# The half-size token block of the last stage: first instead of last, and the last drain in two halves

## The chip, the cores and the metric

The kernel runs on one core of one Trainium2 chip. The metric is the device time of one execution in microseconds (us). A core has a matrix engine (TensorE, called PE in the profile; its weight loads are PEld), VectorE (DVE), ScalarE (ACT), GpSimd (POOL) and a queue engine (SyncE, SP), which issues the transfers between the chip's memory (DRAM) and the on-chip buffers; 16 DMA engines carry them. Each engine works through its own instructions in order and waits for others by semaphores.

## The reference

An attention layer feeds a gated layer, and that feeds a second feed-forward layer. Only the last product of the second feed-forward layer is touched by the change.

```
def _moe2_ref(x, w_in, w_out) -> np.ndarray:
    h = x @ w_in
    g = h - np.tanh(h)
    return (g @ w_out).astype(np.float32)
```

Here x has 2304 tokens x 512, w_in is 512 x 2048 and w_out is 2048 x 512; all is float32.

## The kernel before

The program has a chain of stages: attention with the gated layer's first products, the gated layer's output product, the product `x @ w_in` with the tanh (function `hmm`), and last the product `g @ w_out`, which starts 855.74 us into the span and is called the last stage here. Products are made in pieces: each float32 operand is split into a high and a low part, and three matmuls (high by high, high by low, low by high) replace one.

**The last stage** uses a seven-product scheme for 2 x 2 blocks (Strassen's, in Winograd's form): rows 0 to 1151 and rows 1152 to 2303 of the tokens are the two block rows, the two halves of the 2048 inner columns and of the 512 outer columns are the other blocks. The tokens of each half are cut into blocks `s` of `TB` = 256, of which there are `NSB` = 5: four of 256 and one of 128, since 1152 = 4 x 256 + 128. The inner columns are cut into `MP` = 8 chunks `p`. A step is one pair (s, p); steps run over p inside s, 40 in all, and are numbered 0 to 39 here in the order in which they run.

A step of a 256-token block makes 42 matmuls (7 products x 2 token groups of 128 x 3 matmuls, lines 1023 to 1025), one of the 128-token block 21. The seven products of a block gather in seven PSUM banks over the eight steps, in the order 1, 2, 6, 7, 5, 4, 3. At a block's eighth step `drain` empties each bank as soon as its product is complete: bank 1 by an ACT copy (line 994), the others by seven DVE additions (line 979), of which four are results; `ostore` (line 984) stores those four. The next block's products start in the same banks, so they wait for these drains.

Each step needs prepared operands: `sprep` makes them two steps ahead. `sload` (line 916, three transfers on SP) brings four blocks of g from DRAM into a tile `g2` (two buffers); `sprep` then forms sums on POOL (lines 929, 931) and DVE (lines 930, 933), the high parts `sh` on ACT (lines 932 for the first three operands, 935 for the other four) and the low parts `sl` on DVE (lines 934 and 936). `sh` and `sl` have two buffers each, so ACT's line 932 for step i+2 waits until PE has finished step i. At its end `sprep` calls `sload` for two steps later still, which takes the `g2` buffer that line 934 was the last to read. The first two calls of `sprep` come during the end of the stage ahead, and the loop calls it once behind each step's matmuls (and drains).

**The weights** of w_out lie converted in DRAM, 1792 KB for each p. Those of p = 0 to 2 stay on the chip from earlier; those of p = 3 to 7 are fetched by `wload` (line 942) into memory that the stage ahead gives up, four during its last 16 of 20 products and that of p = 7 behind its last one. They share the SP queue with the loads of g and with the stores of h (line 893), from which g is read back.

Of the kernel before, what the change touches and what calls it, by code (L numbers as in the profile page):

```python
# [13 lines left out]
ALU = mybir.AluOpType  # L14

B, H, S, D = 4, 8, 576, 64
NT, DM = B * S, H * D
# [26 lines left out]
TB = 256  # L44
DG = 2
NSB = -(-(NT // 2) // TB)
# [18 lines left out]
def attention_moe_moe2(ctx: ExitStack, tc: tile.TileContext, kqT, v, s, wg, wv, wo, win, wo2, out):  # L65
    nc = tc.nc
    PE, ACT, DVE, POOL, SP = nc.tensor, nc.scalar, nc.vector, nc.gpsimd, nc.sync
# [169 lines left out]
    g2scr = [dram.tile([128, NT], F, name=f"h{m}") for m in range(M2)]  # L237
# [424 lines left out]
    for i in range(n + LN + 2):  # L662
        u, t = steps[i] if i < n else (None, None)
        b, G, h = units[u] if i < n else (None, None, None)
        first = i < n and t == GRP[G][2][0]
        k = min(share.pop(0) if share and i < n else 1, len(mq))
# [48 lines left out]
        elif i < n and G == 1:  # L715
            s = t - 2 if h % 2 == 0 else t
# [117 lines left out]
    for i, (blk, m) in enumerate(order):  # L834
        w = BLKS[blk][1]
# [5 lines left out]
        for d in range(KD):  # L841
            c = slice(d * 128, d * 128 + 128)
            PE.matmul(acc[d], won[m][0][:, c], gh, start=(m == 0), stop=False)  # L843
            PE.matmul(acc[d], won[m][1][:, c], gh, start=False, stop=False)  # L844
        for d in range(KD):
            c = slice(d * 128, d * 128 + 128)
# [30 lines left out]
    def hmm(i):  # L877
# [14 lines left out]
        DVE.tensor_tensor(out=th, in0=ps, in1=th, op=ALU.subtract)  # L892
        SP.dma_start(out=g2scr[MO[j]][:, a:a + w], in_=th)

    def dwidth(s):
        return min(TB, NT // 2 - s * TB)

    def d_open():
        cv_left.close()
        DP["g"] = ctx.enter_context(tc.tile_pool(name="dg", bufs=2, side="left"))  # L900
        DP["s"] = ctx.enter_context(tc.tile_pool(name="ds", bufs=2, side="right"))
        for i in range(DG):
            sload(i)

    def sload(i):
        if i >= NSB * MP:
            return
        s, p = divmod(i, MP)
        tb = dwidth(s)
        g = S_["g", i] = DP["g"].tile([128, 4, TB], F, tag="g2", name="g2", bufs=DG)  # L910
        for f, (m, t0) in enumerate(((p, NT // 2), (p, 0), (p + MP, 0), (p + MP, NT // 2))):
            if f == 3:
                continue
            k = 2 if f == 2 else 1
            src = g2scr[m].rearrange("p (a t) -> p a t", a=2)[:, t0 // (NT // 2):t0 // (NT // 2) + k, s * TB:s * TB + tb]
            SP.dma_start(out=g[:, f:f + k, 0:tb], in_=src)

    def sprep():
        i = S_["i"]
        if i >= NSB * MP:  # L920
            return
        S_["i"] += 1
        tb = dwidth(i // MP)
        g = S_.pop(("g", i))[:, :, 0:tb]
        t = DP["g"].tile([128, 4, TB], F, tag="s4", name="s4", bufs=2)[:, :, 0:tb]
        sh = DP["s"].tile([128, 7, TB], R, tag="sh", name="sh")[:, :, 0:tb]
        sl = DP["s"].tile([128, 7, TB], R, tag="sl", name="sl")[:, :, 0:tb]
        a21, a11, a12, a22 = (g[:, f] for f in range(4))
        POOL.tensor_tensor(out=t[:, 0], in0=a21, in1=a22, op=ALU.add)  # L929
        DVE.tensor_tensor(out=t[:, 2], in0=a11, in1=a21, op=ALU.subtract)  # L930
        POOL.tensor_tensor(out=t[:, 1], in0=t[:, 0], in1=a11, op=ALU.subtract)
        ACT.activation(out=sh[:, 0:3], in_=g[:, 1:4], func=AF.Copy)  # L932
        DVE.tensor_tensor(out=t[:, 3], in0=a12, in1=t[:, 1], op=ALU.subtract)
        DVE.tensor_tensor(out=sl[:, 0:3], in0=g[:, 1:4], in1=sh[:, 0:3].bitcast(F), op=ALU.subtract)  # L934
        ACT.activation(out=sh[:, 3:7], in_=t, func=AF.Copy)
        DVE.tensor_tensor(out=sl[:, 3:7], in0=t, in1=sh[:, 3:7].bitcast(F), op=ALU.subtract)
        sload(i + DG)
        S_["s", i] = sh, sl
# [31 lines left out]
    op = ctx.enter_context(tc.tile_pool(name="op", bufs=1, side="left"))  # L970
    acc = {}

    def otile(k, w):
        pool = w2 if k[1:].isdigit() else fp if k[0] == "t" else op
        return pool.tile([128, 512], F, tag=k, name="o")[:, 0:w]

    def dadd(k, x, y, w, op=ALU.add):
        o = otile(k, w)
        DVE.tensor_tensor(out=o, in0=x, in1=y, op=op)
        return o  # L980

    def ostore(s, lo_tok, half, o, w):
        r0 = (0 if lo_tok else NT // 2) + s * TB
        SP.dma_start(out=out[r0:r0 + w // 2, half * 256:half * 256 + 256].rearrange("(a p) c -> p a c", p=128),
                     in_=o.rearrange("p (a c) -> p a c", c=256))

    R_ = {}

    def drain(s, n, w):
        par = s % 2  # L990
        a = acc[n]
        if n == 1:
            R_["c1"] = otile("o00", w)
            ACT.activation(out=R_["c1"], in_=a, func=AF.Copy)
        elif n == 2:
            ostore(s, True, 0, dadd(("th0", "th1")[par], a, R_["c1"], w), w)
        elif n == 6:
            R_["u2"] = dadd("o01", a, R_["c1"], w)
        elif n == 7:
            R_["u3"] = dadd("o10", a, R_["u2"], w)  # L1000
        elif n == 5:
            ostore(s, False, 1, dadd(("th2", "th3")[par], a, R_["u3"], w), w)
            R_["v"] = dadd("o11", a, R_["u2"], w)
        elif n == 4:
            ostore(s, False, 0, dadd(("th4", "th5")[par], a, R_["u3"], w), w)
        else:
            ostore(s, True, 1, dadd(("ox0", "ox1")[par], a, R_["v"], w), w)

    wload(MP - 1)
    for i, (s, p) in enumerate(dsteps):  # L1010
        tb = dwidth(s)
        nt = tb // 128
        if p == 0:
            for n in OORD:
                acc[n] = bank(n, [128, nt * 256])
        sh, sl = S_.pop(("s", i))
        w = WO[p]
        for n in OORD:
            g, f = OG[n], OW[n]
            for t in range(nt):  # L1020
                o = acc[n][:, t * 256:t * 256 + 256]
                c = slice(t * 128, t * 128 + 128)
                PE.matmul(o, sh[:, g, c], w[:, 0, f], start=(p == 0 and t == 0), stop=False)  # L1023
                PE.matmul(o, sh[:, g, c], w[:, 1, f], start=False, stop=False)  # L1024
                PE.matmul(o, sl[:, g, c], w[:, 0, f], start=False, stop=(p == MP - 1 and t == nt - 1))  # L1025
            if p == MP - 1:
                drain(s, n, nt * 256)
        sprep()
# [43 lines left out]
```

## Time and profile before

| | |
|---|---|
| time, three runs | 1042.85, 1043.33 (median), 1045.74 us |
| profiled execution: its time, its span | 1044.35 us, 1042.6 us |
| PE busy in the span | 1018.2 us (98%) |
| matmuls of the last stage | 3 x 504 = 1512, from 855.74 to 1038.57 us |
| last DVE instruction ends | 1039.71 us |

The page of the profile gives each engine's busy time, and the trace behind it is read by views: rows of time, waits, windows, transfers. The profiled execution's time is 1.75 us longer than its span, which lies around the program, and 1.02 us above the median of the three runs. Times in the rows count from the start of the span. A name such as `g<-h` reads "tile g is written from tensor h".

### The profile page before, as it was taken

The page shows a single profiled execution, that of the slowest core. Times are in us where ns is not written, and L with a number is a line of the kernel's source. Part 1 is how long each engine was busy: PE and PEld are TensorE (multiplying, and loading weights), DVE is VectorE, ACT ScalarE, POOL GpSimd, SP SyncE. Part 2 cuts the span into 40 slices and gives each one's busy share as a digit, 9 for nine tenths or more (in the row PEclk, how much of TensorE's full clock was granted, in tenths as well). Part 3 has the DMA queues.
Part 4 walks back from the last instruction along what each step waited for, and adds up shares of the span by engine and source line. Part 5 has one row for each costly group of instructions (what it writes and reads, how often), then busy time and mean ns, then how long its engine had stood idle before and what let it go on. Part 6 is the DMA issues. An engine that isn't in the chain of part 4 may idle for free.

```text
span 1042.6 us, 19611 instructions
## 1 busy us (share of the span) xinstructions
PE 1018.2 (98%) x6812; PEld 950.6 (91%) x6812; DVE 636.9 (61%) x1467; ACT 513.6 (49%) x1178; POOL 458.1 (44%) x608
## 2 busy tenths in 40 slices
PE   7898999999999999999999999999999999999997
PEld 5688999999999999999988888888888889999997
DVE  5787667677666566646533444365565245887876
ACT  5876656677656665634432333344444233434333
POOL 3678555677666565513200000055565103453452
PEclk8999999999999999999999999999999999999999
DMA  6674457576565655307634332365787696534433
GB/s 199 212 249 134 131 132 201 163 203 175 165 179 157 166 160 166 105 32 240 217 102 131 112 116 76 117 212 176 263 302 273 245 325 219 151 112 135 145 96 102
DMA packets 109091, 177.09 MB, mean 170 GB/s; under 512 B 16000, under 2 KB 71296, under 8 KB 107712
## 3 DMA queue, kind: packets, MB, share of 16 engines
q1 hardware_dynamic: 108992, 175.85, 54.1%
q8 instruction: 53, 0.87, 0.3%
q14 instruction: 46, 0.38, 0.1%
HBM read 128.79 MB, written 47.00 MB: 169 GB/s over the span
## 4 chain that ended last, share of the span: by engine, by line
PE 88%; DMA 3%; DVE 3%; POOL 2%; issue 2%; ACT 1%; SPq 1%; DVEq 0%; POOLq 0%; ACTq 0%
PE bank L577 9%; PE bank L573 9%; PE bank L574 9%; PE bank L886 6%; PE bank L885 6%; PE bank L889 6%; PE bank L515 5%; PE bank L843 5%; PE bank L844 5%; PE bank L847 5%; PE bank L1025 5%; PE bank L1024 5%; PE bank L1023 5%; PE bank L470 4%; PE bank L411 1%
## 5 line engine op out<-in xcount | busy, mean ns | idle before, releaser
L1025 PE MATMUL bank<-wo,sl 128*128 128x256 f32 x504 | 142.5, 283 | 1.7 <-DVE sl L934 1.5
L1023 PE MATMUL bank<-wo,sh 128*128 128x256 f32 x504 | 141.8, 281 | 0.0
L1024 PE MATMUL bank<-wo,sh 128*128 128x256 f32 x504 | 141.7, 281 | 0.0
L886 PE MATMUL bank<-y,ring 128*128 128x512 f32 (+1 forms) x320 | 115.8, 368 | 0.0
L885 PE MATMUL bank<-y,ring 128*128 128x512 f32 (+1 forms) x320 | 115.7, 368 | 0.0
L892 DVE TENSOR_TENSOR th<-bank,th 128x512 f32<-128x512 f32 (+1 forms) x80 | 50.2, 635 | 92.2 <-ACT th L891 87.9
L115 POOL TENSOR_TENSOR ring<-tmp,ring 128x512 fp32r<-128x512 f32 x16 | 22.7, 1421 | 185.4 <-ACT ring L125 165.2
L494 ACT ACTIVATE pth<-bank 128x384 fp32r<-128x384 f32 (+1 forms) x96 | 45.5, 474 | 113.0 <-PE bank L470 93.0
L1025 PEld LDWEIGHTS bank<-wo,sl 128*128 128x128 f32 x504 | 95.2, 189 | 2.8 <-DVE sl L934 2.1
L929 POOL TENSOR_TENSOR s<-g 128x256 f32<-128x256 f32 (+1 forms) x40 | 34.9, 873 | 140.9 <-DMA g<-h 127.6
L495 DVE TENSOR_TENSOR ptl<-bank,pth 128x384 fp32r<-128x384 f32 (+1 forms) x96 | 51.2, 534 | 72.8 <-ACT pth L494 72.2
L1024 PEld LDWEIGHTS bank<-wo,sh 128*128 128x128 f32 x504 | 95.2, 189 | 0.0
L1023 PEld LDWEIGHTS bank<-wo,sh 128*128 128x128 f32 x504 | 95.2, 189 | 0.0
L800 DVE TENSOR_TENSOR gl<-g,gh 128x512 fp32r<-128x512 f32 (+1 forms) x60 | 37.7, 637 | 84.7 <-PE bank L847 61.9
L438 ACT ACTIVATE sp<-sp,nm 128x128 f32<-128x128 f32 (+4 forms) x144 | 83.4, 579 | 5.3 <-DVE nm L431 5.2
L891 ACT ACTIVATE th<-bank 128x512 f32<-128x512 f32 (+1 forms) x80 | 43.4, 551 | 79.0 <-PE bank L889 76.3
L470 PE MATMUL bank<-ident,sp 128*128 128x128 f32 x400 | 68.4, 275 | 11.5 <-POOL sp L454 4.6
L799 ACT ACTIVATE gh<-g 128x512 fp32r<-128x512 f32 (+1 forms) x60 | 35.0, 591 | 90.4 <-PE bank L844 79.6
L889 PE MATMUL bank<-y,ring 128*128 128x512 f32 (+1 forms) x320 | 78.7, 368 | 0.0
L932 ACT ACTIVATE sh<-g 128x768 fp32r<-128x768 f32 (+1 forms) x40 | 31.2, 780 | 86.6 <-PE bank L1024 59.5
L342 POOL TENSOR_TENSOR kl<-kq,kh 128x576 fp32r<-128x576 f32 (+1 forms) x48 | 57.6, 1200 | 29.7 <-ACT kh L341 29.0
L886 PEld LDWEIGHTS bank<-y,ring 128*128 128x128 f32 x320 | 60.3, 189 | 10.2
(385 smaller groups left out, 3169.4 us busy)
## 6 DMA issues: line engine op xcount, KB each, us to landing
h<-th SPq DMA_DIRECT2D x64, 256.0 KB, 2.6
kq<-in_kq SPq DMA_DIRECT2D x32, 448.0 KB, 3.7
raw<-in_wo SPq DMA_DIRECT2D x28, 512.0 KB, 5.0
g<-g SPq DMA_DIRECT2D x48, 256.0 KB, 2.7
g<-h SPq DMA_DIRECT2D x72, 128.0 KB, 2.3
w<-wst SPq DMA_DIRECT2D x5, 1792.0 KB, 6.3
wo<-w SPq DMA_DIRECT2D x5, 1792.0 KB, 8.6
cbc<-cum SPq DMA_DIRECT2D x32, 256.0 KB, 5.2
```

Of the source, the lines that this page charges most:

```text
L342: POOL.tensor_tensor(out=kl, in0=d["k"], in1=kh.bitcast(F), op=ALU.subtract)
L438: ACT.activation(out=e["sp"], in_=e["sp"], func=AF.Exp, scale=-1.0, bias=e["m"], accum_out=e["sum"])
L470: PE.transpose(e["tr"][j // 4][:, j % 4, :], e["sp"][:, c:c + 128], ident)
L573: PE.matmul(ps, wh[:, c], xh[:, k], start=(k == 0), stop=False)
L574: PE.matmul(ps, wl[:, c], xh[:, k], start=False, stop=False)
L577: PE.matmul(ps, wh[:, c], xl[:, k], start=False, stop=(k == KD - 1))
L885: PE.matmul(ps, wh[:, c], yh[k], start=(k == 0), stop=False)
L886: PE.matmul(ps, wl[:, c], yh[k], start=False, stop=False)
L889: PE.matmul(ps, wh[:, c], yl[k], start=False, stop=(k == KD - 1))
L1023: PE.matmul(o, sh[:, g, c], w[:, 0, f], start=(p == 0 and t == 0), stop=False)
L1024: PE.matmul(o, sh[:, g, c], w[:, 1, f], start=False, stop=False)
L1025: PE.matmul(o, sl[:, g, c], w[:, 0, f], start=False, stop=(p == MP - 1 and t == nt - 1))
```

## The change

The block of 128 tokens becomes block 0, and blocks 1 to 4 have 256. `dstart(s)` gives the first token of a block. So steps 0 to 7 now have 21 matmuls and load 64 KB blocks of g where they had 42 and 128 KB, and steps 32 to 39 have 42 where they had 21. The last drain of the last block, which is now 512 columns wide, is made as two additions of 256 columns, each with a store of its own. Beside that one more addition and one more store, the number of operations, the order in which each engine takes them, and the weight transfers stay as they were. Line numbers from 895 to 1010 rise by 5 or so, and those of the last loop by 10.

```diff
+    short = NT // 2 % TB
+
     def dwidth(s):
-        return min(TB, NT // 2 - s * TB)
+        return TB if s else short
+
+    def dstart(s):
+        return s * TB - (TB - short) * (s > 0)
...
-            src = g2scr[m].rearrange("p (a t) -> p a t", a=2)[:, t0 // (NT // 2):t0 // (NT // 2) + k, s * TB:s * TB + tb]
+            src = g2scr[m].rearrange("p (a t) -> p a t", a=2)[:, t0 // (NT // 2):t0 // (NT // 2) + k, dstart(s):dstart(s) + tb]
...
-    def ostore(s, lo_tok, half, o, w):
-        r0 = (0 if lo_tok else NT // 2) + s * TB
+    def ostore(s, lo_tok, half, o, w, t0=0):
+        r0 = (0 if lo_tok else NT // 2) + dstart(s) + t0
...
+        elif s < NSB - 1:
+            ostore(s, True, 1, dadd(("ox0", "ox1")[par], a, R_["v"], w), w)
         else:
-            ostore(s, True, 1, dadd(("ox0", "ox1")[par], a, R_["v"], w), w)
+            o = otile(("ox0", "ox1")[par], w)
+            for c in range(0, w, 256):
+                DVE.tensor_tensor(out=o[:, c:c + 256], in0=a[:, c:c + 256], in1=R_["v"][:, c:c + 256], op=ALU.add)
+                ostore(s, True, 1, o[:, c:c + 256], 256, c // 2)
```

On SP, at the start of the last stage, before the change: the last three stores of h, the weights of p = 7 (`wo27`), and the first two transfers of the g load for step 4 (`h4`, the first of them standing for both).

```order
L893 DMA h14_93<-th2_11150 128x256
L893 DMA h7_86<-th2_11167 128x256
L893 DMA h15_94<-th2_11184 128x256
L942 DMA wo27_11191<-w7_102 128x3584
L916 DMA g2_11253<-h4_83 128x256 x2
L916 DMA g2_11253<-h12_91 128x2x256
```

The same place after the change:

```order
L893 DMA h14_93<-th2_11150 128x256
L893 DMA h7_86<-th2_11167 128x256
L893 DMA h15_94<-th2_11184 128x256
L947 DMA wo27_11191<-w7_102 128x3584
L921 DMA g2_11232<-h4_83 128x128 x2
L921 DMA g2_11232<-h12_91 128x2x128
```

The order is the same; the g load behind the weights has half its width.

On DVE, where block 0 ends and block 1 begins, before the change: the last instruction for step 7, the four that prepare step 8, and the first of the seven drain additions of block 0, which are called in step 7.

```order
L936 TENSOR_TENSOR sl_11529<-s4_11527,sh_11528 128x1024
L930 TENSOR_TENSOR s4_11584<-g2_11481 128x256
L933 TENSOR_TENSOR s4_11584<-g2_11481,s4_11584 128x256
L934 TENSOR_TENSOR sl_11586<-g2_11481,sh_11585 128x768
L936 TENSOR_TENSOR sl_11586<-s4_11584,sh_11585 128x1024
L979 TENSOR_TENSOR o_11613<-bank2_11194,o_11605 128x512
```

The same place after the change:

```order
L941 TENSOR_TENSOR sl_11403<-s4_11401,sh_11402 128x4x128
L935 TENSOR_TENSOR s4_11437<-g2_11376 128x256
L938 TENSOR_TENSOR s4_11437<-g2_11376,s4_11437 128x256
L939 TENSOR_TENSOR sl_11439<-g2_11376,sh_11438 128x768
L941 TENSOR_TENSOR sl_11439<-s4_11437,sh_11438 128x1024
L984 TENSOR_TENSOR o_11460<-bank2_11194,o_11455 128x256
```

The preparation of step 8 keeps its full width and still stands ahead of the drains of block 0, which now have half their width and come from a step of half the length.

## Rows read from the trace of the kernel before

**Rows 1.** Windows: us, busy us (instructions) by engine, granted clock, DMA share, GB/s.

```profile
860.00:880.00 20.00, 19.56 (x164) 19.36 (x164) 10.97 (x14) 7.30 (x8) 4.45 (x6) 1.00 0.69 246
1020.00:1043.00 23.00, 17.28 (x138) 16.52 (x137) 12.91 (x29) 6.68 (x12) 5.56 (x10) 0.98 0.28 82
```

**Rows 2.** Timeline of PE, start and middle of the first block: start, us, instruction, idle before.

```profile
855.74 0.28 PE L1023 MATMUL bank<-wo,sh 128*128 128x256 f32 x1
...
875.91 0.28 PE L1024 MATMUL bank<-wo,sh 128*128 128x256 f32 x1
876.63 0.38 PE L1025 MATMUL bank<-wo,sl 128*128 128x256 f32 x1 [0.44 <-DVE sl L934]
```

**Rows 3.** Timeline of PE, the last block: its first matmul, its longest wait, its end.

```profile
1015.99 0.28 PE L1023 MATMUL bank<-wo,sh 128*128 128x256 f32 x1
...
1023.97 0.28 PE L1024 MATMUL bank<-wo,sh 128*128 128x256 f32 x1
1025.31 0.39 PE L1025 MATMUL bank<-wo,sl 128*128 128x256 f32 x1 [1.06 <-DVE sl L934]
...
1038.29 0.28 PE L1025 MATMUL bank<-wo,sl 128*128 128x256 f32 x1
```

**Rows 4.** Timeline of the SP queue, weights of p = 7, then g of step 4.

```profile
859.23 0.44 SPq L942 DMA_DIRECT2D wo<-w  x1
862.81 1.40 SPq L916 DMA_DIRECT2D g<-h  x3
```

**Rows 5.** Transfers issued 859 to 860 and 862.5 to 864.3: count, KB, us to landing.

```profile
wo<-w SPq DMA_DIRECT2D x1, 1792.0 KB, 12.0
...
g<-h SPq DMA_DIRECT2D x2, 128.0 KB, 8.6
g<-h SPq DMA_DIRECT2D x1, 256.0 KB, 8.8
```

**Rows 6.** Timelines of ACT and DVE (preparation of step 2), then POOL (step 4).

```profile
860.91 0.85 ACT L932 ACTIVATE sh<-g 128x768 fp32r<-128x768 f32 x1 [4.58 <-PE bank L1024]
...
861.79 0.96 DVE L934 TENSOR_TENSOR sl<-g,sh 128x768 fp32r<-128x768 f32 x1 [4.34 <-ACT sh L932]
...
872.62 0.73 POOL L929 TENSOR_TENSOR s<-g 128x256 f32<-128x256 f32 x1 [10.94 <-DMA g<-h]
```

**Rows 7.** Timelines of DVE and POOL, one turn of a g2 buffer at 128 tokens.

```profile
1024.69 0.56 DVE L934 TENSOR_TENSOR sl<-g,sh 128x384 fp32r<-128x384 f32 x1
...
1028.72 0.46 POOL L929 TENSOR_TENSOR s<-g 128x128 f32<-128x128 f32 x1 [2.29 <-DMA g<-h]
...
1029.96 0.55 DVE L934 TENSOR_TENSOR sl<-g,sh 128x384 fp32r<-128x384 f32 x1
1030.74 0.98 DVE L936 TENSOR_TENSOR sl<-s,sh 128x512 fp32r<-128x512 f32 x1 [0.23 <-ACT sh L935]
```

**Rows 8.** Timelines of DVE and POOL, one turn of a g2 buffer at 256 tokens.

```profile
875.08 1.49 DVE L934 TENSOR_TENSOR sl<-g,sh 128x768 fp32r<-128x768 f32 x1
...
880.66 1.00 POOL L929 TENSOR_TENSOR s<-g 128x256 f32<-128x256 f32 x1 [4.90 <-DMA g<-h]
...
884.06 1.78 DVE L936 TENSOR_TENSOR sl<-s,sh 128x1024 fp32r<-128x1024 f32 x1 [0.26 <-ACT sh L935]
```

**Rows 9.** Timeline of DVE, the drains of the fourth and of the last block.

```profile
1013.10 4.66 DVE L979 TENSOR_TENSOR o<-bank,o 128x512 f32<-128x512 f32 x7
...
1036.90 2.81 DVE L979 TENSOR_TENSOR o<-bank,o 128x256 f32<-128x256 f32 x7 [0.20 <-ACT o L994]
```

**Rows 10.** Timeline of PE early in the span: its longest wait.

```profile
18.93 0.77 PE L392 MATMUL bank<-kq 65*128 65x128 f32 x2 [3.18 <-DMA kq<-cumsum]
```

**Rows 11.** Windows around that wait, columns as in rows 1 (clock third from the end).

```profile
18.00:18.50 0.50, 0.00 (x0) 0.00 (x0) 0.00 (x0) 0.00 (x0) 0.50 (x2) 0.70 0.27 65
...
24.50:25.00 0.50, 0.50 (x3) 0.41 (x3) 0.50 (x2) 0.37 (x2) 0.00 (x0) 0.50 0.41 125
25.00:25.50 0.50, 0.50 (x4) 0.38 (x4) 0.35 (x4) 0.21 (x1) 0.00 (x0) 0.98 0.27 83
```

## The prediction

> **What bounds the kernel now.** I read the page first: PE is busy for 98% of the span, so time can only be won where PE waits or has ended. The windows then say where that is in the last stage. From 860 to 880 PE is busy 19.56 of 20 us while the DMA engines are 69% busy; in the last 23 us it is busy 17.28 [rows 1]. The timeline of PE names the gaps. In step 4 the third matmul starts 0.72 us behind the second, because a low part came late, and the one after it is late by another 0.1 [rows 2]. The last block, of 128 tokens, has 168 matmuls; the first starts at 1015.99, the last at 1038.29 [rows 3].
>
> The pitch of matmuls is read from the start: from 855.74 to the second matmul of step 4, at 875.91, there are 169 pitches, so one is 0.119 us [rows 2]. A step of 42 takes 5.01 us, one of 21 takes 2.51. The last block would need 167 x 0.119 = 19.9 us and took 22.3: it loses about 2.4 us to waits, 1.06 of it idle in one place [rows 3] (with a pitch of 0.117, as in undisturbed steps later, 2.7). I take 2.5. So the small block at the end costs 2.5 us and step 4 costs 0.7: this is all that the new order can save inside the stage.
>
> Why do small steps wait? A turn of a `g2` buffer has a length of its own. In the last block line 934 ends at 1024.69 + 0.56 = 1025.25 and frees the buffer; three transfers are issued and land, and POOL starts on them at 1028.72, 3.47 us later; line 934 of that step ends at 1030.51, 1.79 us after that, and line 936 at 1031.72 [rows 7]. A turn is 5.26 us and serves two steps, and two steps of PE take 5.01. The pipeline can't keep up by itself with small steps, and any lateness stays. At 256 tokens the turn is 4.09 us from 876.57 to POOL's start at 880.66 and 5.18 more until line 936 ends at 885.84, 9.3 us in all for two steps of 10.0 [rows 8].
>
> **The start after the change, step by step.** The matmuls are the same 1512, so I follow waits. PE would end steps 0 to 3 at 858.25, 860.75, 863.3 and 865.8, and step 4 would start then, 10 us earlier than it does now.
>
> *When g for step 4 lands.* Its load is issued when line 934 of step 2 is done, and ACT's line 932 ahead of it waits for the end of step 0: now ACT starts at 860.91, line 934 ends at 862.75 and the load goes out at 862.81 [rows 4, 6]. With half steps ACT can go at 858.4 and line 934 is done by about 859.6 (0.85 + 0.56 at most). But the weights of p = 7 stand ahead on SP, and are issued until 859.67 [rows 4]: the load goes out at about 859.7 instead of 862.8. It gains little: those weights took 12.0 us to land, until 871.2, the load of g issued 3.6 us behind them took 8.6 to 8.8, and POOL began on it at 872.62 [rows 5, 6]. It lay behind the weights and came right after them. What is saved is bytes: the load for step 4 and the one for step 3 ahead of it each have 256 KB less, and at the 246 GB/s of these windows [rows 1] that is about 1 us each. I take 1.6 us in all, so POOL starts at 871.0. Bounds: nothing saved gives 872.6; all four loads up to there halved (1 MB, 4 us) gives 868.6.
>
> *From there one chain runs through the loads to block 1.* All durations are those of the turns above [rows 7, 8]:
> - POOL starts at 871.0, line 934 of step 4 ends 1.79 later, 872.8. PE waits for it with the third matmul of step 4: some 7 us of waiting where 0.7 is seen now.
> - That frees the buffer for step 6: POOL starts 3.47 later, at 876.3, and line 934 of step 6 ends at 878.1.
> - That frees the buffer for step 8, the first of 256 tokens: POOL starts 4.09 later, at 882.2, and line 936 ends 5.18 after that, at 887.4.
> - The seven drain additions of block 0 stand behind that line on DVE. The first takes 0.40 (2.81 / 7, [rows 9]), and PE can start product 2 of step 8 in its bank at 887.8.
>
> Without waits PE would be at this matmul at 855.74 + 8 x 2.51 + 6 x 0.119 = 876.5. The start is 11.3 us late. Behind it the drains (0.40 each against 0.7 us for a product's six matmuls) and the turns of 9.3 us are fast enough, and PE runs freely as it does now.
>
> *The clock.* In this trace PE waited for 3.18 us from 15.8 [rows 10]; in the half microsecond from 18.0 the granted clock fell to 0.70, the mean of its two levels 2.4 and 1.2 GHz being in it, it was still 0.50 in the one from 24.5, and 0.98 in the next [rows 11]. A wait of 6 to 7 us ahead of step 4 should do the same, and step 4 then runs at half speed and ends about 2 us later. Most of this lies inside the wait for step 8. Only `sh` of step 6 depends on it (ACT's line 932 needs the end of step 4): that moves the chain by about 0.5 us (bounds 0 and 1).
>
> **The end after the change.** The last step has 42 matmuls, and the 128-token waits are gone: minus 2.5 us, and minus 0.7 for step 4's old wait, already counted in the new one. The tail: DVE now ends 1039.71 - 1038.57 = 1.14 us behind PE [rows 3, 9]. With additions of 4.66 / 7 = 0.67 us [rows 9] and the last in two of 0.40, five full ones run while PE works; the sixth waits for nothing but DVE, and by the sum the second half ends about 1.25 us behind PE. The last store has 128 KB as now, but behind it in the queue lie one of 256 KB and one of 128 KB, and now two of 128. I take +0.4 (bounds 0 and +1.0; 256 KB at 246 GB/s is 1.1). Without the halving the last addition would take 0.67 and its store carry 256 KB, so the halving saves perhaps 0.5, and is in this sum.
>
> **Sum:** 11.3 + 0.5 - 0.7 - 2.5 + 0.4 = +9.0 us. Against the profiled execution's 1044.35 that is 1053.4; the median of the three runs is 1.02 lower, so 1052.3. The bounds of the landing (-2.4, +1.6), the clock (-0.5, +0.5), the tail (-0.4, +0.6) give 1049 to 1055.
>
> **A rule weighed.** In the rows the load of 512 KB took 8.8 us behind the weights [rows 5]. The Trainium skill, page "DMA: Bandwidth & Descriptors", section "Anatomy of one DMA — SWDGE (gpsimd) path", prices a transfer of its other issuing path at about 2.0 us and bytes over 436 GB/s, which by estimate is 2.6 us for the 256 KB load of step 4: by it that load would be there at 863.7, and the change would come out as the first rival below. The same page, section "Queues, rings and completion order", says that descriptors on one DMA engine's ring are taken in order, and the trace agrees: 8.8 us and not 3, right behind the weights.
>
> **Rivals.**
> - *The load isn't held behind the weights* (no loss). If it landed as in the last block, POOL could start at 859.7 + 3.5 = 863.2 and step 4 wouldn't wait. What decides is whether g for step 4 is there by 864. Even so line 934 of step 6 can't end before step 4 does: 868.3 + 0.1 + 0.85 + 0.56 = 869.8. Then 4.09 + 5.18 + 0.40 lead to 879.5 for product 2 of step 8, 3.0 late: 3.0 - 3.2 + 0.4 = +0.2, so 1043.5. Against it: the 8.8 us, and 69% busy DMA engines over 20 us.
> - *Faster.* The same, and the wait at step 8 hidden too: 1043.33 - 3.2 + 0.4 = 1040.5. For this the 256-token turn would have to be 3 us shorter than its 9.3; only the move of the small block out of the drained end speaks for it.
> - *The clock falls again.* At step 8 PE has no more than product 1 to do between about 883.5 or 885.5 and 887.8. A wait of 3.18 us was enough to lose it, one of 1.06 in the last block was not (the window still shows 0.98, with the idle end in it) [rows 1, 3, 10]. This wait lies between. From 18.9 to 25 PE ran at half speed, 6 us that did the work of 3 [rows 10, 11]: +3.0, so 1055.3.
> - *Drains don't hold step 8.* If the banks were free, PE would go as soon as line 934 of step 8 ends, and wait only for line 936 with its fifteenth matmul: about 1.4 us less, 1050.9, inside the forecast's bounds. The order on DVE speaks against it.
>
> **Chances.** The forecast (with the last rival) 0.73, the clock's second fall 0.15, no loss 0.09, faster 0.03. A difference under 0.3% (3.1 us) is about what a measurement of this kernel can't tell from none. The first two cases are slower: 0.88; within 0.3%: 0.09; faster: 0.03. The range runs from 1047.0, between the forecast's lower bound and the case without loss, to 1055.5, which takes in the clock's second fall.
>
> **What would show it.** Right: PE idle for 5 to 7 us ahead of step 4's third matmul, put down to DVE line 939 with POOL released by the DMA; the load for step 4 issued near 859.7 and landing 10 to 11 us later, right after the weights; the granted clock at 0.5 behind it; a second wait around step 8, with drains behind line 941 on DVE; hardly a wait in the last 25 us. Wrong: if step 4's g lands before 866, the main term falls; if it lands but step 8 doesn't wait, the turn at 256 tokens was over-sized; if the last block still loses 2 us, the saving wasn't one of the block's size.

## The result, and the profile after

The changed kernel takes 1053.22 us (median of six runs, 1051.80 to 1055.09), the kernel before 1043.76 us (six runs on the same chips): a ratio of 1.0087, 95% interval 1.0072 to 1.0103. It is 0.9% slower; the forecast was 1052.3 us, in a range of 1047.0 to 1055.5. Of all the runs below one, of the kernel whole_drain, stands alone with 1673.74 us at a mean granted clock of 0.557; it is left out of that kernel's ratio, and without it the kernel's median is 1053.50 us.

The profiled execution took 1053.11 us with a span of 1051.3 us. Its last stage begins 1.4 us earlier than in the one before (854.34 against 855.74, [rows 2]). The change touches no more ahead of it than the first loads and preparations, and the kernels of this study that have small first loads start the stage anywhere from 853.30 to 855.62. So stages are compared here by their own length, from the start of their first matmul to the start of their last: 1038.29 - 855.74 = 182.55 us before [rows 2, 3], 1046.39 - 854.34 = 192.05 us after. That is +9.50; the tail from there to the end of the span adds 4.91 - 4.31 = 0.60.

The view of waits of PE, after, from 845 us on; columns are who waited for whom, us in total, times, longest:

```profile
PE bank L1033 <- ACT sh L937: 4.6, 1, 4.6
PE bank L1033 <- ACT o L999: 1.2, 1, 1.2
PE bank L1035 <- DVE sl L939: 1.1, 1, 1.1
PE bank L1033 <- DVE o L984: 0.5, 1, 0.5
```

The timeline of PE has these four waits, the stage's first and last matmul, and the place of each:

```profile
854.34 0.28 PE L1033 MATMUL bank<-wo,sh 128*128 128x256 f32 x1
...
869.10 0.39 PE L1033 MATMUL bank<-wo,sh 128*128 128x256 f32 x1 [4.56 <-ACT sh L937]
...
870.66 0.58 PE L1035 MATMUL bank<-wo,sl 128*128 128x256 f32 x1 [1.05 <-DVE sl L939]
...
884.55 0.38 PE L1033 MATMUL bank<-wo,sh 128*128 128x256 f32 x1 [1.24 <-ACT o L999]
...
886.06 0.39 PE L1033 MATMUL bank<-wo,sh 128*128 128x256 f32 x1 [0.53 <-DVE o L984]
...
1046.39 0.28 PE L1035 MATMUL bank<-wo,sl 128*128 128x256 f32 x1
```

The first two are the first and the third matmul of step 4, the other two are products 1 and 2 of step 8. Behind them nothing waits: step 9 to the end runs at 5.0 us a step, and the last eight steps, which had lost 2.4 us as a small block [rows 3], lose nothing.

Who was late is read on the SP queue and in the landings. First the SP timeline, then the transfers issued from 856.5 to 857 and from 858 to 859.7 (count, KB, us to landing):

```profile
856.59 0.38 SPq L947 DMA_DIRECT2D wo<-w  x1
858.16 1.65 SPq L921 DMA_DIRECT2D g<-h  x3
```

```profile
wo<-w SPq DMA_DIRECT2D x1, 1792.0 KB, 11.0
...
g<-h SPq DMA_DIRECT2D x2, 64.0 KB, 9.6
g<-h SPq DMA_DIRECT2D x1, 128.0 KB, 9.3
```

The weights of p = 7 land at 856.59 + 11.0 = 867.6. The load of g for step 4, a seventh of their size, goes out 1.6 us behind them, takes over 9 us too, and is there for POOL at 868.58. Timelines of POOL and of DVE then show the chain from that load to step 8:

```profile
868.58 0.46 POOL L934 TENSOR_TENSOR s<-g 128x128 f32<-128x128 f32 x1 [11.29 <-DMA g<-h]
...
875.06 0.46 POOL L934 TENSOR_TENSOR s<-g 128x128 f32<-128x128 f32 x1 [4.13 <-DMA g<-h]
...
881.12 0.74 POOL L934 TENSOR_TENSOR s<-g 128x256 f32<-128x256 f32 x1 [3.03 <-DMA g<-h]
```

```profile
870.06 0.55 DVE L939 TENSOR_TENSOR sl<-g,sh 128x384 fp32r<-128x384 f32 x1
...
876.29 0.55 DVE L939 TENSOR_TENSOR sl<-g,sh 128x384 fp32r<-128x384 f32 x1
...
884.26 1.41 DVE L941 TENSOR_TENSOR sl<-s,sh 128x1024 fp32r<-128x1024 f32 x1 [0.25 <-ACT sh L940]
885.59 2.79 DVE L984 TENSOR_TENSOR o<-bank,o 128x256 f32<-128x256 f32 x7
```

The three POOL rows are steps 4, 6 and 8: each starts when its load has landed, and each load went out when DVE's line 939 of two steps earlier had freed the buffer. The drains of block 0 begin at 885.59, right behind line 941 of step 8, and PE's product 2 follows at 886.06.

Windows by stretch (busy us by engine, granted clock third from the end) show the clock's part:

```profile
870.00:876.00 6.00, 5.34 (x25) 5.34 (x26) 3.06 (x8) 2.20 (x4) 1.72 (x3) 0.50 0.32 90
876.00:883.00 7.00, 7.00 (x58) 7.00 (x58) 3.96 (x9) 2.53 (x4) 2.87 (x5) 0.95 0.51 150
883.00:887.00 4.00, 2.23 (x16) 1.81 (x15) 3.54 (x7) 2.06 (x3) 2.34 (x2) 0.98 0.35 93
887.00:890.00 3.00, 3.00 (x16) 3.00 (x15) 3.00 (x7) 0.37 (x1) 1.34 (x2) 0.50 0.68 231
```

In this execution it fell twice to the lower level (0.50): behind the wait for step 4, and again in step 8, where PE made 16 matmuls in 3 us in place of some 25.

### The profile page after: what moved, and what is told of

It is laid out like the page before. It is cut to its first block, busy times and chain, and to the rows that moved or that the text cites. A ratio compares the mean times of both kernels' runs of the same rounds, so it can differ in the third digit from the quotient of the medians.

```text
span 1051.3 us, 19614 instructions
## 1 busy us (share of the span) xinstructions
PE 1020.2 (97%) x6812; PEld 952.9 (91%) x6812; DVE 639.4 (61%) x1468; ACT 513.3 (49%) x1178; POOL 464.3 (44%) x608
## 4 chain that ended last, share of the span: by engine, by line
PE 89%; DMA 3%; POOL 2%; DVE 2%; ACT 1%; issue 1%; SPq 1%; DVEq 0%; POOLq 0%; ACTq 0%
PE bank L577 9%; PE bank L573 9%; PE bank L574 9%; PE bank L886 6%; PE bank L885 6%; PE bank L889 6%; PE bank L1033 5%; PE bank L1034 5%; PE bank L1035 5%; PE bank L515 5%; PE bank L843 5%; PE bank L844 5%; PE bank L847 5%; PE bank L470 4%; PE bank L411 1%; PE bank L410 1%
## 5 line engine op out<-in xcount | busy, mean ns | idle before, releaser
L1033 PE MATMUL bank<-wo,sh 128*128 128x256 f32 x504 | 144.1, 286 | 6.3 <-ACT sh L937 4.6
L1034 PE MATMUL bank<-wo,sh 128*128 128x256 f32 x504 | 143.7, 285 | 0.0
L1033 PEld LDWEIGHTS bank<-wo,sh 128*128 128x128 f32 x504 | 97.2, 193 | 6.9 <-ACT sh L937 4.8
L934 POOL TENSOR_TENSOR s<-g 128x256 f32<-128x256 f32 (+1 forms) x40 | 38.7, 967 | 137.8 <-DMA g<-h 137.2
L1034 PEld LDWEIGHTS bank<-wo,sh 128*128 128x128 f32 x504 | 97.3, 193 | 0.0
L470 PE MATMUL bank<-ident,sp 128*128 128x128 f32 x400 | 68.3, 275 | 11.6 <-POOL sp L454 4.2
L886 PEld LDWEIGHTS bank<-y,ring 128*128 128x128 f32 x320 | 60.3, 189 | 10.1
```

The source lines that it names most:

```text
L470: PE.transpose(e["tr"][j // 4][:, j % 4, :], e["sp"][:, c:c + 128], ident)
L886: PE.matmul(ps, wl[:, c], yh[k], start=False, stop=False)
```

## The experiments

The theory was that of the forecast: the load for step 4 waits behind the last weights, and a chain of buffer turns carries the lateness to step 8. The rival was that a small block costs by its own short steps, wherever it stands but last; beside it the clock, the drains and the halved store had to be priced. Every kernel was timed beside the kernel before on the same chip, but not all on one chip: the kernel before took 1043.76 us beside the changed kernel, 1044.04 beside w7_out, w67_out, third and warm, 1043.06 beside dg3_after, dg3_before, drains_first and whole_drain, and 1044.53 beside dg4_after and dg4_before. So kernels of different groups are best compared by their ratios. The table has the median, the ratio to before with its interval, and the length of the last stage in the profiled execution (first to last matmul).

| kernel | median us | ratio (95%) | stage us |
|---|---|---|---|
| before | 1043.76 | | 182.55 |
| changed | 1053.22 | 1.0087 (1.0072 to 1.0103) | 192.05 |
| w7_out | 1048.36 | 1.0037 (1.0024 to 1.0050) | 1043.19 - 854.36 = 188.83 |
| w67_out | 1046.42 | 1.0018 (1.0008 to 1.0027) | 1039.50 - 855.12 = 184.38 |
| third | 1048.52 | 1.0038 (1.0026 to 1.0051) | 1040.42 - 854.37 = 186.05 |
| warm | 1051.86 | 1.0070 (1.0057 to 1.0082) | 1045.33 - 854.79 = 190.54 |
| dg3_after | 1047.79 | 1.0042 (1.0030 to 1.0054) | 1041.12 - 854.01 = 187.11 |
| drains_first | 1054.70 | 1.0108 (1.0092 to 1.0124) | 1045.82 - 855.58 = 190.24 |
| whole_drain | 1053.91 | 1.0103 (1.0086 to 1.0121) | 1046.96 - 855.62 = 191.34 |
| dg4_after | 1044.72 | 1.0003 (0.9991 to 1.0015) | 1035.83 - 853.30 = 182.53 |
| dg3_before | 1038.97 | 0.9962 (0.9948 to 0.9975) | 1034.65 - 855.55 = 179.10 |
| dg4_before | 1039.32 | 0.9965 (0.9951 to 0.9978) | 1033.39 - 854.30 = 179.09 |

**Without the last weights (w7_out).**

```diff
-    wload(MP - 1)
+    WO[MP - 1] = WO[0]
```

> The changed kernel without the transfer of the weights of p = 7 (the steps of p = 7 use the weights of p = 0, so that part of the product is another one). Theory, the load of g for step 4 waits behind these weights and a chain runs from it to step 8: the load then follows the weights of p = 6 and lands about 5 us earlier; product 2 of step 8 starts about 5.5 us late against a stage without waits, where it is 10.9 late in the changed kernel, and the second fall of the clock goes: 1046 to 1047.5 us. Rival, the small block costs what it does because of its own short steps, wherever the weights are: 1051 us or more.

Step 4 waited 0.64 us for ACT and 1.03 for DVE instead of 4.56 and 1.05. Timelines of POOL (step 4) and of PE (product 2 of step 8):

```profile
864.65 0.45 POOL L934 TENSOR_TENSOR s<-g 128x128 f32<-128x128 f32 x1 [6.19 <-DMA g<-h]
```

```profile
882.36 0.58 PE L1033 MATMUL bank<-wo,sh 128*128 128x256 f32 x1
```

POOL began 864.65 - 854.36 = 10.29 us into the stage, 3.95 earlier than in the changed kernel where about 5 was expected, and product 2 of step 8 came 28.00 into it, 7.2 late where 5.5 was expected. The clock fell in this execution as well, in step 4 (0.73 from 864 to 870) and again at step 8, after a wait of 2.42 us; step 8 took 8.0 us. 1048.4 lies 0.9 us above the expected 1046 to 1047.5. How much of that is the chain and how much the second fall is open: the run at the median has a mean clock of 0.998, the profiled one, at 1049.65 us, 0.993. It is 2.6 us below what the rival needs.

**Without the last two weights (w67_out).**

```diff
-        if i > n2 and (i - n2) % NW == 0:
+        if i > n2 and (i - n2) % NW == 0 and i < n2 + 4 * NW:
             wload(ND + (i - n2) // NW - 1)
...
-    wload(MP - 1)
+    WO[MP - 1], WO[MP - 2] = WO[0], WO[1]
```

> The changed kernel without the transfers of the weights of p = 6 and p = 7 (those steps use the weights of p = 1 and p = 0). Theory: the load of g for step 4 lands within 4 us of its issue, step 4 does not wait, the granted clock stays at 1.00, and only the turn into the first block of 256 tokens is left, about 3 us: 1043.5 to 1045 us. Rival, short steps at the start cost by themselves: 1050 us or more.

The transfers issued from 857 to 860.5, in this kernel (as above):

```profile
g<-h SPq DMA_DIRECT2D x2, 64.0 KB, 1.9
g<-h SPq DMA_DIRECT2D x1, 128.0 KB, 2.4
```

The same load lands in 1.9 to 2.4 us where it took 9.3 to 9.6. Step 4 does not wait, steps 0 to 6 take 2.5 to 2.6 us each, and one wait is left in the whole stage, on product 1 of step 8. Its row in PE's timeline, and the windows around it:

```profile
877.85 0.38 PE L1033 MATMUL bank<-wo,sh 128*128 128x256 f32 x1 [2.15 <-ACT o L999]
```

```profile
875.00:878.00 3.00, 0.85 (x7) 0.65 (x7) 1.74 (x3) 1.75 (x4) 1.68 (x4) 1.00 0.35 94
878.00:881.00 3.00, 2.89 (x13) 2.60 (x14) 2.79 (x7) 0.53 (x1) 1.56 (x1) 0.53 0.63 180
```

Product 2 of step 8 starts at 879.36, 24.24 us into the stage, where one without waits has it at 8 x 2.51 + 0.71 = 20.8: 3.4 us late, of which the rival "the load isn't held" had 3.0. On top of it the clock falls, against the expectation, and step 8 takes 6.9 us. Of the 1.9 us too much, 0.8 lie ahead of product 2, which DVE's first drain holds anyway, and 1.1 behind it. The median, 1046.4, is 1.4 us above the expected 1045. The theory holds for the weights; the rival's 1050 is excluded.

**The small block third of five (third).**

```diff
-        return TB if s else short
+        return TB if s != 2 else short
...
-        return s * TB - (TB - short) * (s > 0)
+        return s * TB - (TB - short) * (s > 2)
```

> The half-size block third of five (steps 16 to 23), all else as in the changed kernel; nothing is left out. Theory: no weights are in flight there, so the wait of 6 us and the falls of the clock are gone; step 4 waits its 0.7 us as before the change; the block loses some 1 us by its own turns, and about 3 us where the next block of 256 tokens begins, because its first load and preparation take 9.3 us: 1043.5 to 1046.5 us. Rival, a small block that is not last costs 9 us wherever it stands: 1052 us.

PE's waits in this kernel:

```profile
PE bank L1033 <- ACT o L999: 1.8, 1, 1.8
PE bank L1035 <- DVE sl L939: 0.8, 1, 0.8
```

No weights are near, and the block still loses: steps 16 to 22 take 19.8 us in place of 17.6, product 1 of the block behind waits 1.8 us, the clock falls again, and step 24 takes 6.9:

```profile
959.00:962.00 3.00, 2.89 (x14) 2.59 (x15) 2.79 (x7) 0.57 (x1) 2.15 (x2) 0.57 0.63 157
```

Measured is 4.5 us over before, 2 above the expected bound: the fall was not in the sum. So with two buffers a small block that has 256-token blocks behind it does cost more than one at the end: its stage is 3.5 us longer than before, against 9.5 with the block first. The rival is right in part; it falls as the main cause: of the 9.5 us that the stage is longer with the block first, taking the weights away (w67_out) leaves 184.38 - 182.55 = 1.83.

**The clock kept up (warm).**

```diff
+        d = {4: 50, 8: 20}.get(i, 0)
+        for j in range(d):
+            if j == 0:
+                idle = bank(0, [128, 256])
+            PE.matmul(idle, WO[0][:, 0, 0, 0:128], WO[0][:, 0, 0], start=(j == 0), stop=(j == d - 1))
```

> The changed kernel with 50 extra matmuls ahead of step 4 and 20 ahead of step 8, on operands that are there, into a bank that nobody reads; they fill most of the two waits. Theory: the clock stays at 1.00, steps 4, 5 and 8 run at full speed, but the chain through loads and preparation hardly moves: about 0.5 us from the first fall and 1.6 from the second come back, 1051 us. Rival, the fallen clock is most of the loss: 1047 us or less. Rival, the clock costs nothing since the waits hide it: 1053 us.

The window in which the changed kernel ran at a clock of 0.71, here:

```profile
872.00:880.00 8.00, 7.99 (x65) 7.59 (x64) 5.42 (x13) 2.95 (x5) 2.64 (x5) 1.00 0.46 131
```

Steps 4 to 6 took 8.2 us in place of 11.6, yet product 2 of step 8 started at 885.64, 30.85 into the stage, against 31.72: most of what the faster steps gave (the extra matmuls also fill what was a wait inside step 4) went into a longer wait for step 8. The stage is 1.5 us shorter, the median 1.4. That is what the theory gave, and the rival with 1047 falls. The times alone hardly exclude the one with 1053, since the intervals of the two ratios overlap (1.0057 to 1.0082 here, 1.0072 to 1.0103 for the changed kernel); it is the steps, one execution of each, that speak against it.

**Three and four g2 buffers (dg3, dg4; the diff for 3, on either kernel).**

```diff
-DG = 2
+DG = 3
```

> The changed kernel with three g2 buffers in place of two, so each load goes out a step earlier. Theory, the load waits behind the weights only because the buffer comes free so late: the load for step 4 now goes out ahead of the weights of p = 6 and p = 7, and step 4 does not wait; the load for step 5 is the first behind the weights of p = 7, and step 5 waits about 3 us; step 8 starts about 5 us late instead of 10.9, perhaps with a fall of the clock: 1046.5 to 1049 us. Rival, the number of buffers does not matter since the transfers are short of bandwidth there: 1052 us or more.

Now step 4 does not wait. Step 5 does, whose load is the first behind the weights of p = 7 (PE's timeline):

```profile
869.89 0.45 PE L1033 MATMUL bank<-wo,sh 128*128 128x256 f32 x1 [3.18 <-ACT sh L937]
```

Product 2 of step 8 starts 28.25 into the stage, 7.4 late where 5 was expected, since the clock fell in step 5 (0.50 from 873 to 876): step 5 took 5.75 us, and ACT's line 937 of step 7 could start only behind it, at 875.72. The time is in the expected range, and the rival falls.

> The kernel before with three g2 buffers, the small block last. Theory, the last block loses its 2.5 us because a turn of a buffer (5.26 us) is longer than two short steps: with a third buffer this loss and the 0.7 us of step 4 go, 1040.5 to 1042 us, faster than both kernels. Rival, the drains of the fourth block on DVE make the last block late, and not the buffer: 1043.5 us.

In the kernel before with a third buffer no wait of PE is left in the stage. Windows of the two places that lost time [rows 1], and the first and last matmul of the stage in PE's timeline:

```profile
860.00:880.00 20.00, 20.00 (x171) 20.00 (x170) 14.11 (x16) 7.19 (x8) 6.72 (x8) 1.00 0.74 264
...
1016.00:1039.00 23.00, 18.93 (x160) 18.72 (x159) 15.66 (x36) 7.73 (x14) 5.79 (x10) 0.98 0.33 98
```

```profile
855.55 0.28 PE L1023 MATMUL bank<-wo,sh 128*128 128x256 f32 x1
...
1034.65 0.28 PE L1025 MATMUL bank<-wo,sl 128*128 128x256 f32 x1
```

The last eight steps take 2.46 to 2.55 us each. The stage is 182.55 - 179.10 = 3.45 us shorter: close to the 2.5 + 0.7 that the forecast found to be saved, saved by a buffer instead of by a new order. 1038.97 us is below the expected 1040.5 and is the fastest version of the study beside dg4_before; the rival (the drains) falls.

> The changed kernel with four g2 buffers. Theory, all waits at the start come from loads that go out too late: the loads for steps 4 and 5 now go out ahead of the last weights, those for steps 6 and 7 land with some 1 us to spare or lack, step 8 starts about 1 us late with no fall of the clock: 1039.5 to 1042 us, faster than before, but not faster than the small block last with as many buffers. Rival, the small block first has a cost of its own that loads do not make: 1046 us or more.

> The kernel before with four g2 buffers. Theory: three already leave no wait in the last stage, so the fourth adds nothing: 1039 to 1040 us. Rival, loads still wait for buffers somewhere: 1 us or more faster than with three.

With four buffers the small block first has a stage as long as the kernel before (182.53) and a time that cannot be told from it, against the expected 1039.5 to 1042 (the rival had 1046 or more). The clock stays up in the profiled execution, but step 6 still waits for a load behind the weights, as POOL's timeline and PE's show:

```profile
867.80 0.47 POOL L934 TENSOR_TENSOR s<-g 128x128 f32<-128x128 f32 x1 [6.46 <-DMA g<-h]
```

```profile
869.88 0.39 PE L1035 MATMUL bank<-wo,sl 128*128 128x256 f32 x1 [0.96 <-DVE sl L939]
```

Step 8 still waits 0.35 and 0.54 us, and product 2 of step 8 is 2.9 us late. With the small block last the fourth buffer adds nothing (179.09 against 179.10). So the small block first stays 3.4 us longer than last, and the expectation of a time ahead of the kernel before failed. Whether this is a cost of its own, as the rival has it, is not shown: the load for step 6 landed at 867.7, right behind the weights of p = 7 at 867.0, DVE then worked with hardly a break until the drains at 876.51, and the SP queue held the rest of the load for step 8 until those weights had landed (its view of waits has line 921 waiting for landings of weights twice, 6.3 us in all).

**The drains ahead of step 8's preparation (drains_first).**

```diff
-        sprep()
+        if i != MP - 2:
+            sprep()
+        if i == MP - 1:
+            sprep()
```

> The changed kernel with the preparation of step 8 called behind the drains of block 0 and not ahead of them. Theory, the drains of block 0 wait on DVE behind the preparation of step 8 and hold product 2 of step 8: the drains then run while step 7 runs, product 2 can start when product 1 is done, and the wait at step 8 shrinks by about 1.4 us: 1051.5 us. Rival, the preparation itself comes too late and the drains only fill the time: the third matmul of step 8 waits for it instead, 1053 us.

DVE's timeline and PE's:

```profile
881.86 2.81 DVE L984 TENSOR_TENSOR o<-bank,o 128x256 f32<-128x256 f32 x7 [0.63 <-ACT o L999]
...
886.46 1.42 DVE L941 TENSOR_TENSOR sl<-s,sh 128x1024 fp32r<-128x1024 f32 x1 [0.26 <-ACT sh L940]
```

```profile
886.26 0.39 PE L1035 MATMUL bank<-wo,sl 128*128 128x256 f32 x1 [2.37 <-DVE sl L939]
```

The drains are done by 884.67, and PE waits at its third matmul for line 939. Only the name of the wait has changed: product 2 starts at 886.84, 31.26 us into the stage, 0.5 to 0.8 us earlier than in the changed kernel (31.72) or in whole_drain (32.04), not 1.4, and the time is no shorter. The preparation is what comes late.

**The last drain whole (whole_drain).**

```diff
-        elif s < NSB - 1:
+        else:
             ostore(s, True, 1, dadd(("ox0", "ox1")[par], a, R_["v"], w), w)
-        else:
-            o = otile(("ox0", "ox1")[par], w)
...
```

> The changed kernel with the last drain made and stored whole, 512 columns. Theory: the stage is the same, and from the start of the last matmul to the end of the span the profile shows 5.4 us instead of 4.9, since the store has twice the bytes. Rival, the halving is worth nothing or costs: 4.9 us or less. The time itself, 1053 to 1054 us, cannot tell them apart.

The end of DVE's timeline, in this kernel and then in the changed one:

```profile
1043.79 4.71 DVE L984 TENSOR_TENSOR o<-bank,o 128x512 f32<-128x512 f32 x7 [3.49 <-PE bank L1030]
```

```profile
1046.66 0.68 DVE L984 TENSOR_TENSOR o<-bank,o 128x512 f32<-128x512 f32 x1
1047.25 0.75 DVE L1016 TENSOR_TENSOR o<-bank,o 128x256 f32<-128x256 f32 x2
```

DVE ends 1048.50 - 1046.96 = 1.54 us behind the start of the last matmul with the whole addition, 1048.00 - 1046.39 = 1.61 with the halves; from there to the end of the span it is 4.74 us against 4.91. The halves save nothing: DVE is a full addition behind PE at that point, so the first half cannot begin before the whole one would.

## Why the prediction was right, point by point

- **The load for step 4.** It was to go out near 859.7, or 3.96 us into the stage, and POOL to start 15.3 into it. It went out at 3.82 and POOL started at 14.24. Mechanism right, 1.0 us too long: the weights of p = 7 went out 2.25 us into the stage instead of 3.49 as before, and landed 13.2 into it instead of 15.5. w67_out shows the cause: without the weights ahead the same load lands in about 2 us. The price that the forecast weighed and set aside, from the Trainium skill, page "DMA: Bandwidth & Descriptors", section "Anatomy of one DMA — SWDGE (gpsimd) path", 2.6 us by estimate, is near what w67_out shows with nothing ahead (1.9 to 2.4 us for each of the three transfers), and not near the 9.3 to 9.6 us behind the weights.
- **The wait for step 4.** 5 to 7 us were named; 4.56 + 1.05 and the first fall of the clock made step 5 start 20.5 us into the stage in place of 12.6. The place was wrong: the forecast had PE wait ahead of step 4's third matmul for the low part from DVE, but 4.56 us of it stood ahead of the first one, for the high part from ACT, which comes from the same late load.
- **The chain.** From POOL's start in step 4 to product 2 of step 8 it was to be 16.8 us by turns and 0.5 for the clock; it was 886.06 - 868.58 = 17.48. Its parts were off both ways: the turn of step 6's buffer took 4.45 us where 3.47 stood, step 8's preparation 4.55 where 5.18 stood. The 0.5 for the clock was not found where it was put: for step 6 ACT's line 937 was done at 875.61, and line 939 came behind POOL, at 876.29. With the clock kept up (warm) the same stretch still took 1.0 us less, 885.64 - 869.17 = 16.47, mostly by a shorter turn of step 6's buffer (3.69). Product 2 was 31.72 into the stage, 10.9 late; the sum had 11.8.
- **The drains as its last link.** The order on DVE was right, but it cost little: drains_first shows the preparation to be late, nearly as late as the drains it holds.
- **The second fall of the clock** was a rival with a chance of 0.15. It came, at 1.6 us and not 3.0: step 8 took 7.41 us, of which 0.81 were lost ahead of product 2 and 1.6 behind it. This is the term that the forecast lacked, and by luck it made good for the chain's 0.9 too much. The forecast's own case, without a second fall, came in the profiled execution of whole_drain, whose stage is the changed kernel's up to the last drain: product 2 was 32.04 - 20.8 = 11.2 late, the clock stayed up in step 8, and the stage took 191.34 us, 8.8 more than before.
- **What is saved.** 3.2 us were counted: 10.9 + 1.6 - 9.5 = 3.0 is what is left here; dg3_before, where the same waits go, has 3.45.
- **The tail.** +0.4 was put down, +0.60 measured, with a halving that was worth nothing, not 0.5.

Together 10.9 + 1.6 - 3.0 + 0.6 = 10.1 us inside the stage and behind it, where the forecast had 9.0. The profiled executions differ by 8.76, since the later one entered the stage 1.4 us earlier; the medians moved by 9.5.

The other side fails on its first condition: the load was held behind the weights. And even where it was not (w67_out), the kernel was 0.18% slower than before, where the rival had +0.02%: the turn into the first 256-token block and the clock behind it remain.

## What to carry to other kernels

A small block at the end of a stage shows as idle time there, but its steps are short wherever it stands; before it is moved, read what is in flight where it goes, since here a load of 256 KB behind 1792 KB of weights took some 9.5 us instead of some 2. Here the steps were shorter than the turn of their buffers, and another buffer was the direct cure: it gave 0.4% where the new order lost 0.9%. And halving the last store gave nothing here, since the engine that fills it was itself behind. Not tried was to move the weights of p = 7 instead of the loads, so it is not shown whether the small block first can be made faster than last.

## What the runs showed that was not expected

The granted clock fell after short waits in some executions and not in others of nearly the same shape. At the first matmuls of step 8 waits of 2.15 us (w67_out) and 2.42 (w7_out) and one of 1.24 with 0.53 behind it (the changed kernel) were followed by the lower level; a wait of 2.37 us in drains_first was not, nor were 2.37 with 0.53 behind it in whole_drain, as their windows show, first of drains_first, then of whole_drain:

```profile
884.00:886.00 2.00, 0.00 (x0) 0.00 (x0) 2.00 (x6) 0.63 (x1) 0.86 (x2) 1.00 0.69 231
886.00:888.00 2.00, 1.74 (x13) 1.56 (x13) 1.74 (x3) 1.17 (x2) 1.92 (x2) 1.00 0.33 96
888.00:892.00 4.00, 4.00 (x34) 4.00 (x35) 3.74 (x5) 1.55 (x2) 2.09 (x2) 1.00 0.50 151
```

```profile
886.00:888.00 2.00, 1.32 (x9) 1.12 (x9) 1.93 (x3) 0.83 (x2) 1.77 (x2) 1.00 0.49 134
888.00:892.00 4.00, 4.00 (x36) 4.00 (x35) 3.86 (x8) 0.77 (x1) 1.75 (x2) 1.00 0.65 195
```

So the length of a single wait does not tell whether the clock falls, and a forecast can only give the fall a chance: where it came at the first step of a 256-token block behind the small one, it cost 1.1 (w67_out), 1.3 (third), 1.6 (the changed kernel) and 2.2 us (w7_out) behind product 2. What decides it was not settled. It may also be why dg4_after has a median of 1044.72 us when its profiled span (1040.7 us) speaks for some 1042.4: six of its runs, at a mean clock of 0.997 to 0.999, took 1042.16 to 1044.72 us, the other five, at 0.996, 1045.01 to 1046.55. Only the profiled run has a trace, so where the others lost it is open.
